# First loads on two queues, products of zeros ahead of the first turns, and constants made later

## The chip, the cores and the metric

The kernel runs on one core of a Trainium2 chip. The metric is the device time of one launch in microseconds (us), as the median of several runs.

## What is computed

An attention layer with random features is followed by a mixture of experts in which each token goes to one expert.

```python
# attention: q, k, v are (8 batches, 8 heads, 576 tokens, 64); omega is (128, 64)
proj = einsum('bhsd,md->bhsm', x * scale, omega)          # for q and for k
phi  = exp(h - max(h)) / sqrt(128)                        # h = proj - |x|^2/2
kv   = einsum('bhsm,bhsd->bhmd', k_p, v);  z = sum(k_p, axis=2)
num  = einsum('bhsm,bhmd->bhsd', q_p, kv); den = einsum('bhsm,bhm->bhs', q_p, z) + 1e-6
attn = num / den                                          # -> x: (4608, 512)
# experts: 8 of them, 512 -> 1024 -> 512
logits = x @ w_gate;  e = argmax(logits);  gate_w = softmax(logits)[e]
out = gate_w * (relu(x @ w1[e]) @ w2[e])
```

## The kernel before

**Units.** The attention stage (class `Attention`) goes through 72 units in a fixed order: for each of the 8 batches first a unit "rest" (head number -1, the last 64 tokens of all eight heads), then its heads 0 to 7 (512 tokens each). The text calls the first four units R, 0, 1 and 2. What one unit does:

- `unit_a1` (L136) calls `turn` (L146): TensorE transposes the unit's k and q, eight small products with the identity at L151, into the PSUM tile `tr`. There is a single buffer for all turned tiles (`room`, pool `ps_t`), so the next turn waits until the last one is copied out.
- `unit_a2`: VectorE copies `tr` to `th` (L157).
- `unit_b1`: TensorE multiplies `th` by the scaled omega, `omt`, into `pp` (L166). `pp` has two buffers.
- `unit_max`: VectorE takes the row maxima `mx` (L172).
- `unit_exp`: ScalarE takes the exponentials `kp` and `qp`, four instructions each (L180).
- The `qp` are turned back on TensorE (`t`, again L151) and copied by ScalarE to `qt` (L224). TensorE then makes the sums over k and v (`kf`, L206) and the results (`nu`).

**Order.** The loop in `run` (L293) is software-pipelined by hand. In iteration i it issues the turn of unit i+1, the products and maxima of unit i, the `qp` of unit i-1, the turning back of unit i-2, the `kf` of unit i-1, and the `kp` of unit i. The engines of the attention stage keep exactly the order in which the code issues (`manual_schedule`), each with its own queue, so an instruction that waits holds whatever follows it on its engine.

**Setup.** Ahead of the loop the code makes the identity, clears the buffers `xg` and `xgm` (L789), and makes the constants of the routing (`Routing.setup`, L404) on GpSimd, six of them with VectorE: L420 and L450 to L454. `Attention.__init__` loads omega twice (L75), turns it (L77) and scales it on ScalarE into `omt` (L79); it copies the identity 16 times into the gate table `G` (L89) and clears `rv` (L95), on GpSimd. The pool entry `tt` holds the turned omega too, so the first turn waits for L79.

**Loads.** `load(0)` puts every load of the first batch on SyncE's queue (SP), in this order: k and q of unit R (L111, two transfers each, for the two halves of the partitions), k and q of head 0, k and q of head 1, the gate weights into `G` (L124, two), v of heads 0 and 1, v of unit R into `rv` (two, which wait until GpSimd has cleared `rv`), and then k, q and v of heads 2 and 3, 4 and 5, 6 and 7. The loads of the second batch follow on the same queue.

The function `warm` (L688) issues products of a 128x128 bf16 tile of zeros with 512 columns of zeros. Nothing calls it in this kernel.

Of the kernel before, what the change touches and what calls it, by code (L numbers as in the profile page):

```python
# [30 lines left out]
NG = B // 2  # L31
GT = 2 * NJ + 1
NLT = NG * GT
# [7 lines left out]
SCALE = float(D) ** -0.25  # L41
# [16 lines left out]
class Attention:  # L58
    def __init__(self, tc, ctx, ps, io, q, k, v, omega, wg, xs, routing, ident):
        self.tc, self.nc = tc, tc.nc  # L60
        self.q, self.k, self.v, self.xs, self.routing, self.ident = q, k, v, xs, routing, ident
        nc = tc.nc
        pool = lambda n, b, **kw: ctx.enter_context(tc.tile_pool(name=n, bufs=b, **kw))
        self.cp = pool("at_c", 1)
        self.io, self.ps = io, ps
        self.open = ExitStack()
        self.pp = self.open.enter_context(tc.tile_pool(name="ps_a", bufs=2, space=PSUM))
        self.tt = self.open.enter_context(tc.tile_pool(name="ps_t", bufs=1, space=PSUM))
        self.wk = pool("at_wk", 2)
        self.xo = pool("at_x", 2)  # L70
        cp = self.cp

        om = self.wk.tile([P, 2, D], F32, name="om", tag="kp")
        for i in range(2):
            nc.sync.dma_start(om[:, i, :], omega)  # L75
        pt = self.tt.tile([P, 2, 512], F32, name="pt_om", tag="tt")
        nc.tensor.transpose(pt[:, 0, :P], om.rearrange("p a d -> p (a d)"), ident)  # L77
        self.om = cp.tile([P, M], F32, name="omt")
        nc.scalar.mul(self.om, pt[:, 0, :P], SCALE)  # L79

        self.G = cp.tile([P, H, W - 1], F32, name="G")
# [3 lines left out]
        nc.gpsimd.memset(self.eps, EPS)  # L85
        for a in range(2):
# [3 lines left out]
        self.wg = wg  # L90


        self.rv = [[cp.tile([P, NP, D], F32, name=f"rv{i}{a}") for a in range(2)] for i in range(2)]
        for t in self.rv[0] + self.rv[1]:
            nc.gpsimd.memset(t, 0.0)  # L95
        self.st, self.last = {}, {}

    def load(self, b):
# [7 lines left out]
        def rest(nms):  # L106
            for n, src in nms:
                rem = src[b, :, SM:, :].rearrange("(i a) p d -> a p i d", a=2)
                for a in range(2):
                    to = s["vr"][a] if n == 2 else s["kqr"][:, n]  # L110
                    nc.sync.dma_start(to[a * SR:(a + 1) * SR], rem[a])  # L111

        def main(nms, h):
            for nm, src in nms:
                nc.sync.dma_start(s[nm][:, h], src[b, h, :SM, :].rearrange("h (p j) d -> p h j d", j=NJ))
# [3 lines left out]
        if b == 0:  # L119
            main(kq, slice(0, 1))  # L120
            main(kq, slice(1, 2))
            for a in range(2):
                with nc.allow_non_contiguous_dma(reason="gate weights"):
                    nc.sync.dma_start(self.G[a * D:(a + 1) * D, :, D:], self.wg.rearrange("(h d) e -> d h e", d=D))  # L124
            main(v, slice(0, 2))
# [10 lines left out]
    def unit_a1(self, b, h):  # L136

        nc, s = self.nc, self.st[b]
        src = [s["kqr"][:, n] if h < 0 else s["kq"[n]][:, h] for n in range(2)]
        s[("tr", h)] = self.turn(self.next, [x[:, 2 * i:2 * i + 2, :].rearrange("p a d -> p (a d)")  # L140
                                                 for x in src for i in range(2)])
# [4 lines left out]
    def turn(self, pt, blocks):  # L146

        for n, x in enumerate(blocks):
            for a in range(2):
                r = slice(a * SR, (a + 1) * SR)  # L150
                self.nc.tensor.transpose(pt[:, a, n * SR:(n + 1) * SR], x[r], self.ident[r, r])  # L151
        return pt[:, :, :4 * SR].rearrange("p a (n t) -> p a n t", t=SR)
# [140 lines left out]
    def run(self, pre):  # L293
# [8 lines left out]
        for i in range(n):  # L302
# [32 lines left out]
            pre.ahead(i - n)  # L335
            if u1:
                self.next = self.room(f"tr_{i}")
                self.routing.product(self.next[:, 1, 256:])
# [56 lines left out]
class Routing:  # L395
# [8 lines left out]
    def setup(self):  # L404
# [8 lines left out]
        self.EX = t("rt_EX", [P, GT, E + 1])  # L413
        nc.gpsimd.memset(self.EX[:, :, E:], 1e-9)
        nc.gpsimd.memset(self.CU[:, 0, :], 0.0)

        self.iop = t("rt_iop", [P, P])
        self.iob = t("rt_iob", [P, P], BF16)
        nc.gpsimd.iota(self.iop, pattern=[[1, P]], base=0, channel_multiplier=0, allow_small_or_imprecise_dtypes=True)
        nc.vector.tensor_copy(self.iob, self.iop)  # L420
        self.rev = t("rt_rev", [P, E])
        nc.gpsimd.iota(self.rev, pattern=[[-1, E]], base=E, channel_multiplier=0, allow_small_or_imprecise_dtypes=True)
        self.zero = t("rt_zero", [P, P], BF16)
        nc.gpsimd.memset(self.zero, 0.0)
        self.ones = t("rt_ones", [P, P], BF16)
        nc.gpsimd.memset(self.ones, 1.0)
        self.tri = t("rt_tri", [P, P], BF16)
        nc.gpsimd.affine_select(out=self.tri, in_=self.ones, pattern=[[1, P]], compare_op=ALU.is_gt, fill=0.0,
                                base=0, channel_multiplier=-1)
        self.low = t("rt_low", [P, E, E])  # L430
        self.upp = t("rt_upp", [P, E, E])
# [6 lines left out]
        self.fold = t("rt_fold", [P, SR])  # L438
        nc.gpsimd.tensor_copy(self.fold, ident[:, :SR])
        nc.gpsimd.tensor_tensor(out=self.fold, in0=self.fold, in1=ident[:, SR:], op=ALU.add)  # L440
        idi = t("rt_id", [P, NG, GT], I32)
        nc.gpsimd.iota(idi[:, :, :GT - 1], pattern=[[2 * S, NG], [S, 2], [1, NJ]], base=0, channel_multiplier=NJ)
        for a in range(2):
            nc.gpsimd.iota(idi[a * SR:(a + 1) * SR, :, GT - 1:], pattern=[[2 * S, NG]], base=SM + a * S,
                           channel_multiplier=1)
        part = t("rt_part", [P, NLT], I32)
        self.ihi = t("rt_ihi", [P, NLT])
        self.ilo = t("rt_ilo", [P, NLT])
        flat = idi.rearrange("p g s -> p (g s)")
        nc.vector.tensor_single_scalar(part, flat, 6, op=ALU.logical_shift_right)  # L450
        nc.vector.tensor_copy(self.ihi, part)
        nc.vector.tensor_scalar_add(self.ihi, self.ihi, -float(NT // 64))
        nc.vector.tensor_single_scalar(part, flat, 63, op=ALU.bitwise_and)
        nc.vector.tensor_copy(self.ilo, part)  # L454
# [316 lines left out]
class Experts:  # L771
# [6 lines left out]
    def __init__(self, tc, ctx, rt, xs, w1, w2, out, ident, ps):  # L778
# [9 lines left out]
        for x in self.xg:  # L788
            self.nc.gpsimd.memset(x, 0.0)  # L789
# [373 lines left out]
```

## Time and profile before

| | us |
|---|---|
| median of 3 runs | 698.99 (698.91 to 699.36) |
| the profiled execution | 701.15 |
| its span, first to last instruction | 699.3 |
| what lies outside the span | 1.85 |

The attention stage fills about the first 250 us of the span, the experts the rest. In a timeline row stand the start, the duration, the engine, the line, the tile written and the tiles read, with shapes and the number of instructions merged into the row, and in brackets how long the engine was idle ahead of it and what ended that. A row of the DMA issues (SPq) shows the time in which the queue's engine was busy issuing, not the transfer itself.

### The profile page before, as it was taken

What the parts mean: (1) busy time and instruction counts of PE and PEld (TensorE: products, weight loads), DVE (VectorE), ACT (ScalarE), POOL (GpSimd) and SP (SyncE); (2) the same over time, 40 slices, a digit from 0 to 9 for tenths busy, and PEclk for the clock granted to TensorE, in tenths of its full rate; (3) what the DMA queues carried; (4) which work ended last, traced back from release to release, by engine and by line L of the source; (5) the groups of instructions that cost most, each with busy time, mean ns of one, the idle gap of its engine ahead of it and who ended that gap; (6) DMA issues with size and microseconds to landing.
All of it is one profiled execution on the core that took longest, in us unless ns stands there. A gap on an engine that the chain in (4) does not pass through costs nothing. (4 is left out here: it accounts for less than half of the span.)

```text
span 699.3 us, 19723 instructions
## 1 busy us (share of the span) xinstructions
PE 672.8 (96%) x7596; PEld 615.6 (88%) x7596; DVE 372.6 (53%) x738; ACT 359.9 (51%) x1096; POOL 272.4 (39%) x484
## 2 busy tenths in 40 slices
PE   5999999999999999999999999999999999999992
PEld 4999999999898977899899988999898999998891
DVE  4788888888887778532222253422383365422220
ACT  3999999999998944322212262222262263222120
POOL 6455547886887763222112202222231132122020
PEclk9999999999999999999999999999999999999997
DMA  5953836628492124851233247332267338422200
GB/s 160 269 168 114 268 88 191 209 76 252 138 373 73 34 76 138 286 179 64 93 97 108 91 158 241 108 106 71 84 205 242 108 112 320 138 79 61 78 18 21
DMA packets 92432, 99.57 MB, mean 142 GB/s; under 512 B 28943, under 2 KB 72975, under 8 KB 91665
## 3 DMA queue, kind: packets, MB, share of 16 engines
q1 hardware_dynamic: 85744, 78.91, 35.9%
q0 software_dynamic: 6560, 19.03, 8.2%
q8 instruction: 72, 1.18, 0.7%
q14 instruction: 56, 0.45, 0.2%
HBM read 71.06 MB, written 29.51 MB: 144 GB/s over the span
## 5 line engine op out<-in xcount | busy, mean ns | idle before, releaser
L943 PEld LDWEIGHTS p<-xb,w1p 128*128 128x128 f32 x1632 | 198.1, 192 | 1.7 <-issue 0.5
L943 PE MATMUL p<-xb,w1p 128*128 128x256 f32 x1632 | 198.9, 283 | 0.0
L868 PE MATMUL p<-w2p,hh 128*128 128x512 f32 x576 | 177.8, 390 | 0.0
L1014 POOL DMA_INDIRECT out_dram<-ys,idx x38 | 39.4, 1038 | 313.4 <-ACT ys L1013 201.3
L868 PEld LDWEIGHTS p<-w2p,hh 128*128 128x128 f32 x576 | 107.0, 188 | 21.3
L868 PE MATMUL p<-w2p,hl 128*128 128x512 f32 x312 | 117.7, 389 | 0.0
L1013 ACT ACTIVATE ys<-p,gt 128x512 f32<-128x512 f32 x38 | 26.1, 688 | 163.2 <-PE p L868 146.2
L999 DVE SCALAR_TENSOR_TENSOR hl<-p,hh 128x512 fp32r<-128x512 f32 x68 | 46.0, 688 | 80.5 <-ACT hh L995 78.3
L995 ACT ACTIVATE hh<-p 128x512 fp32r<-128x512 f32 x68 | 39.9, 598 | 91.5 <-PE p L943 91.5
L172 DVE TENSOR_REDUCE mx<-pp 128x8 f32<-128x1024 f32 x64 | 78.0, 1218 | 11.4 <-PE pp L166 10.7
L180 ACT ACTIVATE qp<-pp,mx 128x128 f32<-128x128 f32 x256 | 77.4, 438 | 0.0
L180 ACT ACTIVATE kp<-pp,mx 128x128 f32<-128x128 f32 x256 | 74.2, 387 | 4.6 <-DVE de L264 1.1
L166 PE MATMUL pp<-omt,th 64*128 64x128 f32 x1024 | 73.4, 285 | 0.0
L868 PEld LDWEIGHTS p<-w2p,hl 128*128 128x128 f32 x312 | 58.5, 188 | 12.2
L166 PEld LDWEIGHTS pp<-omt,th 64*128 64x128 f32 x1024 | 64.8, 194 | 0.0
L192 POOL TENSOR_TENSOR k<-kp 128x256 f32<-128x256 f32 x64 | 46.6, 728 | 27.7 <-ACT kp L180 21.8
L157 DVE COPY th<-tr 128x512 f32<-128x512 f32 x63 | 43.3, 687 | 6.8 <-PE tr L151 4.8
L927 DVE STREAM_TRANSPOSE xgm<-xq 128x512 f32<-128x512 f32 x18 | 18.9, 1086 | 51.3 <-DMA xq<-pair_rows 51.3
L255 PE MATMUL nu<-kva,qt 128*64 128x73 f32 x1008 | 46.0, 233 | 0.0
L224 ACT COPY qt<-t 128x512 f32<-128x512 f32 x64 | 42.0, 656 | 3.1 <-PE t L151 2.5
L255 PEld LDWEIGHTS nu<-kva,qt 128*64 128x64 f32 x1008 | 36.7, 136 | 4.2
L206 PE MATMUL kf<-kp,v 128*64 128x128 f32 x512 | 39.4, 275 | 0.0
(365 smaller groups left out, 1002.0 us busy)
## 6 DMA issues: line engine op xcount, KB each, us to landing
w1s<-in_moe_w_dram SPq DMA_DIRECT2D x5, 2048.0 KB, 8.8
w2s<-in_moe_w_dram SPq DMA_DIRECT2D x5, 2048.0 KB, 11.0
xq<-pair_rows SPq DMA_DIRECT2D x76, 128.0 KB, 2.9
v<-in_v_dram SPq DMA_DIRECT2D x32, 256.0 KB, 6.4
token_rows<-x SPq DMA_DIRECT2D x8, 1024.0 KB, 8.0
k<-in_k_dram SPq DMA_DIRECT2D x31, 256.0 KB, 5.2
q<-in_q_dram SPq DMA_DIRECT2D x31, 256.0 KB, 5.9
pair_rows<-xg SPq DMA_DIRECT2D x10, 512.0 KB, 2.8
```

The lines of the kernel that those rows point to most:

```text
L157: self.nc.vector.tensor_copy(t.rearrange("p n (a t) -> p a n t", a=2), s[("tr", h)])
L166: nc.tensor.matmul(o[:, a, n, :], t[r, n, :], self.om[r], start=True, stop=True)
L172: self.nc.vector.tensor_reduce(out=mx, in_=s[("pp", h)], axis=AX.X, op=ALU.max, negate=True)
L180: self.nc.scalar.activation(o[:, j, :], p[:, a, 2 * n + i, :], AF.Exp, bias=mx[:, a, 2 * n + i:2 * n + i + 1])
L192: nc.gpsimd.tensor_tensor(out=k2, in0=kp[:, :2, :], in1=kp[:, 2:, :], op=ALU.add)
L206: nc.tensor.matmul(pkv[c * D:(c + 1) * D, :M], vv, kk, start=n < 2, stop=n > 2)
L224: self.nc.scalar.copy(qt.rearrange("p n (a t) -> p a n t", a=2), s[("t2", h)])
L255: nc.tensor.matmul(o[r, j, :], qt[:, j, r], kva[:, h if h >= 0 else 2 * j + a, :], start=True, stop=True)
L868: self.nc.tensor.matmul(p, x, w[:, c, :], start=c == 0 and x is h and w is self.w2h, stop=c == self.NF - 1 and x is l)
L943: return [lambda w=w, x=x, c=c, n=n: self.nc.tensor.matmul(o, w[:, c, f], x[:, c, :], start=n == 0, stop=n == len(ops) - 1) for n, (w, x, ...
L995: self.nc.scalar.activation(a, self.p_1[g], AF.Relu)
L999: self.nc.vector.scalar_tensor_tensor(out=b, in0=self.p_1[g], scalar=0.0, in1=a.bitcast(F32), op0=ALU.max, op1=ALU.subtract)
```

## The change

Omega's second copy goes to ScalarE's queue, and so do, for the first batch alone, the q of unit R, the gate weights, the v of heads 0 and 1 and the v of unit R. Everything else stays on SP's queue, in its old order. The turning and scaling of omega moves behind the issue of the k and q of unit R. Products of zeros (`warm`) are issued on TensorE: five ahead of the turning of omega, two between the turned k and the turned q of unit R, three behind that q. On GpSimd the clearing of `rv` moves ahead of the copies into `G`; the routing's constants and the clearing of `xg` and `xgm` move out of the setup to the end of iteration 0 of `run`, and the six VectorE instructions among the constants move with them: they stand behind the maxima of unit R and ahead of the copy of unit 1's turn. The tile of zeros is cleared first of all. The attention's setup now stands inside the hand-ordered part too.

```diff
-        for i in range(2):
-            nc.sync.dma_start(om[:, i, :], omega)
-        pt = self.tt.tile([P, 2, 512], F32, name="pt_om", tag="tt")
-        nc.tensor.transpose(pt[:, 0, :P], om.rearrange("p a d -> p (a d)"), ident)
+        for i, eng in enumerate((nc.sync, nc.scalar)):
+            eng.dma_start(om[:, i, :], omega)
         self.om = cp.tile([P, M], F32, name="omt")
-        nc.scalar.mul(self.om, pt[:, 0, :P], SCALE)
+
+        def scaled():
+            self.idle = self.pair("idle")
+            self.routing.warm(self.idle[:, 0], 5)
+            pt = self.tt.tile([P, 2, 512], F32, name="pt_om", tag="tt")
+            nc.tensor.transpose(pt[:, 0, :P], om.rearrange("p a d -> p (a d)"), ident)
+            nc.scalar.mul(self.om, pt[:, 0, :P], SCALE)
+        self.scaled = scaled
...
+        self.rv = [[cp.tile([P, NP, D], F32, name=f"rv{i}{a}") for a in range(2)] for i in range(2)]
+        for t in self.rv[0] + self.rv[1]:
+            nc.gpsimd.memset(t, 0.0)
         for a in range(2):
             r = slice(a * D, (a + 1) * D)
             for h in range(H):
                 nc.gpsimd.tensor_copy(self.G[r, h, :D], ident[r, r])
...
-                    nc.sync.dma_start(to[a * SR:(a + 1) * SR], rem[a])
+                    (nc.scalar if b == 0 and n else nc.sync).dma_start(to[a * SR:(a + 1) * SR], rem[a])
...
-                nc.sync.dma_start(s[nm][:, h], src[b, h, :SM, :].rearrange("h (p j) d -> p h j d", j=NJ))
+                (nc.scalar if b == 0 and nm == "v" and not h.start else nc.sync).dma_start(s[nm][:, h], src[b, h, :SM, :].rearrange("h (p j) d -> p h j d", j=NJ))
...
         rest(((0, self.k), (1, self.q)))
         if b == 0:
+            self.scaled()
             main(kq, slice(0, 1))
             main(kq, slice(1, 2))
             for a in range(2):
                 with nc.allow_non_contiguous_dma(reason="gate weights"):
-                    nc.sync.dma_start(self.G[a * D:(a + 1) * D, :, D:], self.wg.rearrange("(h d) e -> d h e", d=D))
+                    nc.scalar.dma_start(self.G[a * D:(a + 1) * D, :, D:], self.wg.rearrange("(h d) e -> d h e", d=D))
...
         s[("tr", h)] = self.turn(self.next, [x[:, 2 * i:2 * i + 2, :].rearrange("p a d -> p (a d)")
-                                                 for x in src for i in range(2)])
+                                                 for x in src for i in range(2)],
+                                     (0, 2, 0, 3) if b == 0 and h < 0 else (0, 0, 0, 0))
...
-    def turn(self, pt, blocks):
+    def turn(self, pt, blocks, busy=(0, 0, 0, 0)):
 
         for n, x in enumerate(blocks):
             for a in range(2):
                 r = slice(a * SR, (a + 1) * SR)
                 self.nc.tensor.transpose(pt[:, a, n * SR:(n + 1) * SR], x[r], self.ident[r, r])
+            self.routing.warm(self.idle[:, 0], busy[n])
...
             self.unit_sum(*u)
             pre.ahead(i - n)
+            if i == 0:
+                self.routing.constants()
+                pre.clear()
...
+    def constants(self):
+        nc, ident = self.nc, self.ident
         nc.gpsimd.memset(self.EX[:, :, E:], 1e-9)
         nc.gpsimd.memset(self.CU[:, 0, :], 0.0)
...
         nc.vector.tensor_copy(self.iob, self.iop)
...
+        nc.vector.tensor_single_scalar(self.part, flat, 6, op=ALU.logical_shift_right)
+        nc.vector.tensor_copy(self.ihi, self.part)
         nc.vector.tensor_scalar_add(self.ihi, self.ihi, -float(NT // 64))
...
+        nc.vector.tensor_single_scalar(self.part, flat, 63, op=ALU.bitwise_and)
+        nc.vector.tensor_copy(self.ilo, self.part)
...
-        for x in self.xg:
-            self.nc.gpsimd.memset(x, 0.0)
+        self.clear = lambda: [self.nc.gpsimd.memset(x, 0.0) for x in self.xg]
...
+        zero = cp.tile([P, P], BF16, name="zero")
+        nc.gpsimd.memset(zero, 0.0)
         ident = cp.tile([P, P], F32, name="ident")
         make_identity(nc, ident)
         rt = Routing(tc, ctx, xs, ident)
+        rt.zero = zero
...
-            at = Attention(tc, c2, ps, io, q, k, v, omega, wg, xs, rt, ident)
-            rt.open(ps, "nu")
             with sched():
+                at = Attention(tc, c2, ps, io, q, k, v, omega, wg, xs, rt, ident)
+                rt.open(ps, "nu")
                 at.run(ex)
```

## Rows read from the trace of the kernel before

**Rows 1.** Stretches: length, busy time of each engine, PEclk, DMA share, GB/s.

```profile
0.00:5.00 5.00, 0.81 (x4) 0.39 (x4) 0.61 (x1) 1.56 (x2) 4.35 (x21) 1.00 0.23 51
5.00:10.00 5.00, 3.33 (x29) 2.77 (x31) 2.50 (x7) 0.00 (x0) 4.71 (x26) 1.00 0.67 158
...
40.00:50.00 10.00, 9.76 (x207) 8.96 (x205) 8.40 (x17) 9.88 (x38) 4.75 (x11) 1.00 0.69 212
```

**Rows 2.** Timeline of units R and 0, up to the first exponentials.

```profile
0.81 1.28 ACT L79 ACT_TABLE_LOAD   x1 [0.81 <-PEq L1150]
...
3.36 0.44 PE L77 MATMUL pt_om<-ident,om 128*128 128x128 f32 x1 [3.36 <-DMA om<-in_omega_dram]
...
4.97 0.90 PE L151 MATMUL tr_first<-ident,kqr 64*128 64x64 f32 x4 [0.32 <-DMA kqr<-in_k_dram]
...
6.70 0.47 PE L151 MATMUL tr_first<-ident,kqr 64*128 64x64 f32 x3 [0.83 <-DMA kqr<-in_q_dram]
...
7.21 0.69 DVE L157 COPY th_-1_229<-tr_first 128x512 f32<-128x512 f32 x1 [0.57 <-PE tr_first L151]
...
7.95 0.48 PE L151 MATMUL tr_second<-ident,k 64*128 64x64 f32 x4 [0.78 <-DVE th_-1_229 L157]
...
8.43 2.02 PE L166 MATMUL pp_-1_242<-omt,th_-1_229 64*128 64x128 f32 x16
...
10.51 1.23 DVE L172 TENSOR_REDUCE mx_-1_251<-pp_-1_242 128x8 f32<-128x1024 f32 x1 [1.13 <-PE pp_-1_242 L166]
...
11.77 1.14 ACT L180 ACTIVATE kp_-1_254<-pp_-1_242,mx_-1_251 128x128 f32<-128x128 f32 x4 [7.64 <-DVE mx_-1_251 L172]
```

**Rows 3.** Timeline of ScalarE: `kp` of unit 0, `qt` of R, `kp` of 2.

```profile
14.00 1.14 ACT L180 ACTIVATE kp<-pp,mx 128x128 f32<-128x128 f32 x4
...
17.37 0.59 ACT L224 COPY qt_-1_360<-t_-1_351 128x512 f32<-128x512 f32 x1 [1.19 <-PE t_-1_351 L151]
...
22.23 1.14 ACT L180 ACTIVATE kp<-pp,mx 128x128 f32<-128x128 f32 x4 [0.55 <-DVE mx L172]
```

**Rows 4.** The stretch between those two `kp`: length, ScalarE busy, PEclk, DMA share, GB/s.

```profile
14.00:22.23 8.23, 5.70 (x20) 1.00 0.97 267
```

**Rows 5.** Timeline of TensorE and VectorE in that stretch.

```profile
13.78 0.48 PE L151 MATMUL tr<-ident,k 64*128 64x64 f32 x4 [1.08 <-DMA k<-in_k_dram]
...
17.01 1.22 DVE L172 TENSOR_REDUCE mx<-pp 128x8 f32<-128x1024 f32 x1 [1.19 <-PE pp L166]
...
19.21 1.60 PE L166 MATMUL pp<-omt,th 64*128 64x128 f32 x16
...
22.26 1.11 PE L166 MATMUL pp<-omt,th 64*128 64x128 f32 x16
```

**Rows 6.** Timeline of SP's queue: the issues of the first loads.

```profile
0.81 0.89 SPq L75 DMA_DIRECT2D om<-in_omega_dram  x2
1.74 1.41 SPq L111 DMA_DIRECT2D kqr<-in_k_dram  x2
3.20 1.27 SPq L111 DMA_DIRECT2D kqr<-in_q_dram  x2
...
6.58 1.29 SPq L124 DMA_DIRECT2D G<-in_moe_w_gate_dram  x2
...
9.21 1.29 SPq L111 DMA_DIRECT2D rv<-in_v_dram  x2
10.56 0.60 SPq L115 DMA_DIRECT2D k<-in_k_dram  x1
```

**Rows 7.** VectorE alone in the stretch that holds its six constants (columns as rows 4).

```profile
3.30:7.10 3.80, 1.73 (x6) 1.00 0.59 146
```

**Rows 8.** Timeline of TensorE: a stream of products with 512 columns.

```profile
284.56 5.63 PE L868 MATMUL p<-w2p,hl 128*128 128x512 f32 x24
```

**Rows 9.** Stretches behind TensorE's last product (columns as rows 1).

```profile
685.00:686.00 1.00, 0.49 (x3) 0.07 (x1) 0.00 (x0) 0.34 (x1) 0.00 (x0) 1.00 0.08 16
...
689.00:690.00 1.00, 0.00 (x0) 0.00 (x0) 0.00 (x0) 0.00 (x0) 0.00 (x0) 0.61 0.00 0
```

More of the change, by code (lines that the diff above doesn't have):

```diff
@@ L85, in __init__ @@
         nc.gpsimd.memset(self.eps, EPS)
+        self.wg = wg
+        self.rv = [[cp.tile([P, NP, D], F32, name=f"rv{i}{a}") for a in range(2)] for i in range(2)]
+        for t in self.rv[0] + self.rv[1]:
+            nc.gpsimd.memset(t, 0.0)
         for a in range(2):
@@ L89, in __init__ @@
                 nc.gpsimd.tensor_copy(self.G[r, h, :D], ident[r, r])
[L90 to L95, printed above, removed]
         self.st, self.last = {}, {}
@@ L413, in setup @@
         self.EX = t("rt_EX", [P, GT, E + 1])
+        self.iop = t("rt_iop", [P, P])
+        self.iob = t("rt_iob", [P, P], BF16)
+        self.rev = t("rt_rev", [P, E])
+        self.ones = t("rt_ones", [P, P], BF16)
+        self.tri = t("rt_tri", [P, P], BF16)
+        self.low = t("rt_low", [P, E, E])
+        self.upp = t("rt_upp", [P, E, E])
+        self.fold = t("rt_fold", [P, SR])
+        self.idi = t("rt_id", [P, NG, GT], I32)
+        self.part = t("rt_part", [P, NLT], I32)
+        self.ihi = t("rt_ihi", [P, NLT])
+        self.ilo = t("rt_ilo", [P, NLT])
+    def constants(self):
+        nc, ident = self.nc, self.ident
         nc.gpsimd.memset(self.EX[:, :, E:], 1e-9)
         nc.gpsimd.memset(self.CU[:, 0, :], 0.0)
-        self.iop = t("rt_iop", [P, P])
-        self.iob = t("rt_iob", [P, P], BF16)
         nc.gpsimd.iota(self.iop, pattern=[[1, P]], base=0, channel_multiplier=0, allow_small_or_imprecise_dtypes=True)
         nc.vector.tensor_copy(self.iob, self.iop)
-        self.rev = t("rt_rev", [P, E])
         nc.gpsimd.iota(self.rev, pattern=[[-1, E]], base=E, channel_multiplier=0, allow_small_or_imprecise_dtypes=True)
-        self.zero = t("rt_zero", [P, P], BF16)
-        nc.gpsimd.memset(self.zero, 0.0)
-        self.ones = t("rt_ones", [P, P], BF16)
         nc.gpsimd.memset(self.ones, 1.0)
-        self.tri = t("rt_tri", [P, P], BF16)
         nc.gpsimd.affine_select(out=self.tri, in_=self.ones, pattern=[[1, P]], compare_op=ALU.is_gt, fill=0.0,
                                 base=0, channel_multiplier=-1)
-        self.low = t("rt_low", [P, E, E])
-        self.upp = t("rt_upp", [P, E, E])
         nc.gpsimd.memset(self.low, 1.0)
@@ L437, in setup @@
                                 base=0, channel_multiplier=0)
-        self.fold = t("rt_fold", [P, SR])
         nc.gpsimd.tensor_copy(self.fold, ident[:, :SR])
         nc.gpsimd.tensor_tensor(out=self.fold, in0=self.fold, in1=ident[:, SR:], op=ALU.add)
-        idi = t("rt_id", [P, NG, GT], I32)
-        nc.gpsimd.iota(idi[:, :, :GT - 1], pattern=[[2 * S, NG], [S, 2], [1, NJ]], base=0, channel_multiplier=NJ)
+        nc.gpsimd.iota(self.idi[:, :, :GT - 1], pattern=[[2 * S, NG], [S, 2], [1, NJ]], base=0, channel_multiplier=NJ)
         for a in range(2):
-            nc.gpsimd.iota(idi[a * SR:(a + 1) * SR, :, GT - 1:], pattern=[[2 * S, NG]], base=SM + a * S,
+            nc.gpsimd.iota(self.idi[a * SR:(a + 1) * SR, :, GT - 1:], pattern=[[2 * S, NG]], base=SM + a * S,
                            channel_multiplier=1)
[L446 to L451, printed above, removed]
+        flat = self.idi.rearrange("p g s -> p (g s)")
+        nc.vector.tensor_single_scalar(self.part, flat, 6, op=ALU.logical_shift_right)
+        nc.vector.tensor_copy(self.ihi, self.part)
         nc.vector.tensor_scalar_add(self.ihi, self.ihi, -float(NT // 64))
-        nc.vector.tensor_single_scalar(part, flat, 63, op=ALU.bitwise_and)
-        nc.vector.tensor_copy(self.ilo, part)
+        nc.vector.tensor_single_scalar(self.part, flat, 63, op=ALU.bitwise_and)
+        nc.vector.tensor_copy(self.ilo, self.part)
     def open(self, ps, tag):
```

## The prediction

> **What bounds the kernel now.** The change touches only the first 20 us or so, so I first ask whether a microsecond won there reaches the end. The table of stretches says it does: from 40 to 50 us ScalarE is busy 9.88 of 10 us [rows 1]. The units pass one after the other at the pace of that engine, nothing there is tied to the clock on the wall, and the experts start when the attention is through. What counts is the moment from which ScalarE runs without gaps.
>
> The timeline shows that moment: the `kp` of unit 2 at 22.23 [rows 3]. Ahead of it the reader is to see three stretches. Up to 11.77 ScalarE has nothing to do, because a chain runs through the loads, the turn, the copy, the products and the maxima of unit R [rows 2]. TensorE waits in turn for omega (3.36), for k (4.97) and for q (6.70) [rows 2], and the DMA engines are busy only 0.23 of the first 5 us [rows 1]: the loads are late because one queue issues them one by one, 0.45 us for each omega, about 0.7 us for each half of k and q [rows 6]. Then, from the `kp` of unit 0 at 14.00 to that of unit 2 at 22.23, ScalarE is busy 5.70 of 8.23 us [rows 4]; it waits for TensorE (the turned `t`, 1.19 us) [rows 3]. TensorE is late there for two reasons. It waited 1.08 us for the k of unit 2, issued only at 10.56, behind the issue of `rv` [rows 5, 6]. And it is slow: sixteen products of L166 take 2.02 us at 8.43, 1.60 us at 19.21 and 1.11 us at 22.26 [rows 2, 5]. The clock column says 1.00 in all these stretches [rows 1, 4], but the pace is that of the lower level (1.2 GHz) until about 20 us and of the upper one (2.4 GHz) behind it. The durations decide here. Ahead of the rise the engine had worked from 13.78 on with only short pauses.
>
> **The change, part by part.** I follow the chain of unit R with TensorE at the lower level.
>
> *Loads on two queues.* SP issues omega (0.45 us) and the two k (1.41) from 0.81 on, done at 2.7; in the trace the second k lands 1.8 us behind the end of its issue (3.15 to 4.97) [rows 2, 6], so now at 4.5. ScalarE issues the other omega and the two q (0.45 + 1.27) by 2.5; the second q landed 2.2 us behind its issue (4.47 to 6.70), so now at 4.8. An issue from ScalarE does not occur in the trace; I take SP's durations. Below: no cheaper than these. Above: the same row kinds up to twice as long if two queues hinder each other, which would put k at 5.6 and cost 1.1 us.
>
> *Products of zeros.* Twenty-four products with 512 columns take 5.63 us at the upper level, 0.235 each [rows 8]; with the ratio 2.02/1.11 that is 0.43 at the lower. Another shape of bf16 with 512 columns the trace doesn't have; the range is 0.235 to 0.43. Five of them fill 1.05 to 3.2, in which TensorE waited for omega anyway (until 3.36 before): nothing. Turned omega then takes 0.44, to 3.65, and its scaling is done at about 4.1, ahead of the k. The k turns run 4.5 to 4.75 (eight turns take 0.48, 7.95 to 8.43 [rows 2]). Two products end at 5.6; they hide a q that lands up to then, otherwise they cost 0.8. The q turns end at 5.85, the copy `th` starts 0.25 later and ends at 6.8 (0.69 [rows 2]). Three products end at 7.15, so they hold the second turn by 0.35 us.
>
> *Chain to the maxima.* Second turn to 7.65; products of R 7.65 to 9.5; maxima start 2.08 behind the start of the products (8.43 to 10.51 [rows 2]), so at 9.75, and end at 10.95. Before: 11.74. Won so far: 0.8 us.
>
> *The constants on VectorE.* The six instructions, 1.73 us [rows 7], lay in VectorE's idle time before the first copy. Now they are queued behind the maxima of R, and behind them wait the copy of unit 1's turn and with it the maxima of unit 0, for which ScalarE waits. They read what GpSimd makes; GpSimd's whole setup, 4.35 + 4.71 us of work [rows 1], ends by about 10 in either order, so VectorE needn't wait for it. The copy starts at 12.7 and ends at 13.35, the maxima of unit 0 at 14.55. The `kp` of unit 0 comes at 14.55, against 14.00: **0.55 later**, the early loads notwithstanding.
>
> *What follows.* From there the gaps go. The k and q of heads 2 and 3 are issued at 4.8 instead of 10.56, and landed 3.2 us behind that (13.78) [rows 5, 6]; at 8 to 9 they are far ahead of unit 2's turn, which now waits until 13.4 for the copy of unit 1's, since both use the one room. TensorE by then has worked from 4.5 to about 11 nearly without a pause, so I take its clock to have risen by about 10. Then that turn takes 0.25 and the products of unit 1 take 1.1; the maxima of unit 1 end at 16.5, the `qt` of R can start at 16.6, the maxima of unit 2 end at 19.8: each is ready as ScalarE comes to it. ScalarE's work between the two `kp` is 5.70 us [rows 4], some 0.5 less if the ends of its instructions overlap as they do in streams (`kp` 14.00 to `qp` 15.02 while the row shows 1.14 [rows 3]). The `kp` of unit 2 comes between 19.75 and 20.25, against 22.23: **2.0 to 2.5 us won; I take 2.2.**
>
> *The rest, at nothing.* The clearing of `xg` and the constants on GpSimd lie ahead of its first sum, which needs the `kp` of unit 0; GpSimd is free at 10, 4 us earlier. The scaling of omega is needed at 7.65. The second batch's loads are issued some 6 us earlier and come behind the first batch's on the same queue. The copies into `G`, now behind the clearing of `rv`, are read only behind the `kp` of unit 0.
>
> By the Trainium skill ("ScalarE: Activation LUTs", Step-by-step: what each stage is for) the activation table is loaded right before the first instruction that needs it. The trace shows the load at 0.81, 1.28 us, on an idle engine [rows 2], which decides nothing about issues standing ahead of it. Placed first, it would put the second q at 6.1, 0.5 us behind the two products, and take 0.3 to 0.5 us from the 2.2.
>
> **Sum.** Span 699.3 - 2.2 = 697.1; with the 1.85 us around it 698.95, against 701.15 for the profiled execution. The median of the runs lies 2.16 below that execution, so the forecast is 696.8. If the clock rises by 8.5, the products of R take 1.1 instead of 2.0: 3.1 won, 695.9. With late issues, 1.1 less at worst: 697.9.
>
> **The rivals.**
>
> *The clock does not rise early, or falls again.* Behind unit 0's products TensorE would stand idle from about 10 to 12.7 and work sparsely until 16. At the end of the kernel it did its last product in the first half of the stretch from 685, did none behind it, and the clock fell within the stretch from 689 [rows 9]; here products come again after 2.7 us, but few. If the lower level holds until 20 as before, the products of unit 1 end at 15.9 and those of unit 2 at 20.2, its maxima at 21.6: 0.6 won, 698.4. Speaking for it: the clock rose only after a long dense stretch before. The Trainium skill ("TensorE: Matmul & The Clock Gate", Part 4: PE-mode transpose) says that transposes don't count as work for the gate; by that the turns here bring nothing to the rise and only the ten products and L166 do. No row separates the two.
>
> *The sharing brings nothing*, because the transfers land no earlier from a second queue. Then q comes at 6.7 as before, three products hold the second turn to 8.25 and the `kp` of unit 0 comes at 15.5; without the later gaps 1.1 us is still won: 697.9. Against it: the DMA engines were idle three quarters of the time [rows 1].
>
> *ScalarE is held by its own issues: slower.* It issues eight transfers; five (gate weights, v, `rv`) come behind the scaling of omega, 1.29 + 0.6 + 1.29 = 3.2 us (the v priced like the k at 10.56 [rows 6]), from 3.9 to 7.1. Its first `kp` is due at 10.95, 3.8 us later, and another 1.6 us are spare between that and the `kp` of unit 0 (14.55, less two groups of 1.02). So issues up to 2.7 times as long as SP's cost nothing; from 3.4 times on all that was won is gone. At four times they end at 16.7, 5.75 behind 10.95: less the 1.6 and the 2.2 that is 2.0 slower, 701.0. For it: no row shows what an issue costs on ScalarE. Against: the DMA engines that it feeds are not full then (0.23, 0.67 [rows 1]).
>
> *What is won is lost downstream*: some later point waits for something that didn't move. 699.0. The waits of the attention stage show none.
>
> **How the numbers follow.** Forecast 0.64 (695.9 to 697.3, up to 697.9 with late issues); clock 0.15 (698.4, from 697.4 to 698.8); sharing 0.07; ScalarE held 0.07; lost downstream 0.07. 0.2% is 1.4 us, about what a measurement of this kernel tells from no change; so "faster" is below 697.6. To it go the forecast nearly whole (0.62), a fourth of the clock's cases (0.04) and a fourth of the sharing's (0.02): 0.68. Slower: ScalarE held, 0.07. Same: 0.25. The range 695.6 to 698.7 takes in the forecast with its bounds, the clock and the sharing, and leaves out the last two, 0.14.
>
> **What would show it.** Five products at 1.05; turned k at about 4.5; first `kp` near 11; `kp` of unit 0 no earlier than 14, behind six VectorE instructions; then ScalarE gapless and `kp` of unit 2 near 20; L166 in 1.1 us from unit 1 on. Wrong, if L166 still takes 2 us at 14, if ScalarE's issues reach past 10, or if the `kp` of unit 0 comes well before 14 (then the constants cost less than I say).

## The result: 5.9 us slower, and the profile after

The changed kernel takes 704.9 us as the median of 6 runs (703.96 to 705.36), beside 698.96 for the kernel before (698.9 to 699.36): a ratio of 1.0081, with a 95% interval of 1.007 to 1.0092. The forecast was 696.8. Executions of one and the same kernel differ here by some microseconds (those of the kernel before lay between 697.2 and 702.5 in all that were timed), so below each time stands beside runs of the kernel before on the same chip.

The profiled execution of the changed kernel took 704.19 us with a span of 702.3; the one of before had 701.15 and 699.3, and lies 2.2 above its median, so the two traces differ by 3.0 us of span where the medians differ by 5.9. The first view is ScalarE's timeline in the changed kernel (start, duration, engine, line; ACTq is ScalarE issuing a transfer):

```profile
1.27 1.38 ACTq L116 DMA_DIRECT2D kqr<-in_q_dram  x2
2.68 1.28 ACT L83 ACT_TABLE_LOAD   x1 [2.68 <-issue]
3.97 0.28 ACT L83 ACTIVATE omt<-pt_om 128x128 f32<-128x128 f32 x1
8.81 2.36 ACTq L130 DMA_DIRECT2D G<-in_moe_w_gate_dram  x2
12.01 0.39 ACTq L120 DMA_DIRECT2D v<-in_v_dram  x1
13.56 2.60 ACTq L116 DMA_DIRECT2D rv<-in_v_dram  x2
16.21 1.14 ACT L188 ACTIVATE kp_-1_242<-pp_-1_230,mx_-1_239 128x128 f32<-128x128 f32 x4 [11.96 <-DMA v<-in_v_dram]
...
18.22 1.19 ACT L188 ACTIVATE kp<-pp,mx 128x128 f32<-128x128 f32 x4
...
25.34 1.14 ACT L188 ACTIVATE kp<-pp,mx 128x128 f32<-128x128 f32 x4 [0.49 <-DVE mx L180]
```

Omega is scaled at 4.25. Then ScalarE computes nothing for 12 us. Its five later issues come out at 8.81 (and a second gate transfer behind that), 12.01 and 13.56, and its first `kp` at 16.21, against 11.77 before [rows 2]. The bracket of that row names a DMA, not the maxima. The row of the maxima shows that they were not the reason (VectorE's timeline, with the first constant and the copy behind the last):

```profile
10.27 1.23 DVE L180 TENSOR_REDUCE mx_-1_239<-pp_-1_230 128x8 f32<-128x1024 f32 x1 [0.26 <-PE pp_-1_230 L174]
11.41 0.22 DVE L443 CAST rt_iob<-rt_iop 128x128 bf16<-128x128 f32 x1
...
12.37 0.68 DVE L165 COPY th<-tr 128x512 f32<-128x512 f32 x1
```

They ended at 11.50, so ScalarE was held 4.7 us beyond them. Further on the `kp` of unit 0 comes at 18.22 (14.00 before, [rows 3]), and that of unit 2 at 25.34 (22.23 before). The 3.1 us by which it is late reach the end. The last product of the experts starts, in TensorE's timeline of before, at 685.11,

```profile
685.11 0.39 PE L868 MATMUL p<-w2p,hl 128*128 128x512 f32 x1
```

and in that of the changed kernel 2.95 later:

```profile
688.06 0.39 PE L878 MATMUL p<-w2p,hl 128*128 128x512 f32 x1
```

TensorE's timeline shows the second loss. In this execution the clock had risen early, as forecast, since the products of R take 1.13 us at 9.09 against 2.02 before [rows 2]. Then TensorE ran out of work, and the products of unit 1 take 2.08 again:

```profile
1.07 2.31 PE L703 MATMUL idle<-zero 128*128 128x512 bf16 x5 [1.07 <-POOL zero L1137]
...
5.44 0.47 PE L158 MATMUL tr_first<-ident,kqr 64*128 64x64 f32 x3 [0.73 <-DMA kqr<-in_k_dram]
...
9.09 1.13 PE L174 MATMUL pp_-1_230<-omt,th_-1_217 64*128 64x128 f32 x16
...
18.44 2.08 PE L174 MATMUL pp<-omt,th 64*128 64x128 f32 x16 [4.86 <-ACT qp_-1_319 L188]
```

Here the clock column shows it too (stretches of 1 us: length, busy time of PE, PEld, DVE, ACT, POOL, then PEclk, DMA share and GB/s):

```profile
15.00:16.00 1.00, 0.00 (x0) 0.00 (x0) 0.00 (x0) 0.00 (x0) 0.00 (x0) 0.97 1.07 256
16.00:17.00 1.00, 0.00 (x0) 0.00 (x0) 0.00 (x0) 0.79 (x4) 0.00 (x0) 0.50 0.95 201
...
22.00:23.00 1.00, 1.00 (x14) 0.67 (x15) 0.00 (x0) 1.00 (x5) 0.00 (x0) 0.61 0.69 168
23.00:24.00 1.00, 1.00 (x22) 0.97 (x22) 0.69 (x1) 1.00 (x6) 0.81 (x2) 1.00 1.00 339
```

The engine did nothing from 13.6 to 18.44, the granted clock fell to the lower level (0.50 of full speed) at about 16, and it rose again between 22 and 23.

What ScalarE waited for is found in the compiled program, in which every instruction stands with the semaphores for which it waits. In this program each transfer signals its completion on one of eight semaphores (DMAHW0 to 7). They are handed out in turn, over both queues together, and an issue that gets one of them again first waits until the transfer that had it has landed. For the changed kernel, ScalarE's and SP's instructions in order:

```
ACT 4  L83  ACTIVATE omt            [waits PE]
ACT 5  L130 DMA G                   [waits DMAHW2]
ACT 6  L130 DMA G                   [waits DMAHW3]
ACT 7  L120 DMA v heads 0-1         [waits DMAHW5]
ACT 8  L116 DMA rv00                [waits DMAHW7, Pool]
ACT 9  L116 DMA rv01                [waits DMAHW1, Pool]
ACT 10 L188 ACTIVATE kp of R        [waits DVE]
SP 7  k heads 2-3 [DMAHW2]    SP 11 q heads 4-5 [DMAHW6]
SP 8  q heads 2-3 [DMAHW3]    SP 12 v heads 4-5 [DMAHW7]
SP 9  v heads 2-3 [DMAHW4]    SP 13 k heads 6-7 [DMAHW0]
SP 10 k heads 4-5 [DMAHW5]    SP 14 q heads 6-7 [DMAHW1]
```

The five issues have DMAHW2, 3, 5, 7 and 1: the semaphores that SP's k and q of heads 2 and 3, k and v of heads 4 and 5 and q of heads 6 and 7 have just taken. ScalarE therefore can't issue the gate weights, which nobody needs yet, before 256 KB of k have landed, nor the second half of `rv` before the q of heads 6 and 7 has, and its exponentials stand behind all that. The trace keeps the semaphores' events too, and with them the moment at which each of those transfers had landed (the last of its sixteen events):

| ScalarE's issue | the transfer it waits for | landed at (us) | the issue starts at (us) |
|---|---|---|---|
| first G | k of heads 2 and 3 | 8.79 | 8.81 |
| second G | q of heads 2 and 3 | 10.55 | 10.57 |
| v of heads 0 and 1 | k of heads 4 and 5 | 11.98 | 12.01 |
| first half of rv | v of heads 4 and 5 | 13.48 | 13.56 |
| second half of rv | q of heads 6 and 7 | 15.49 | 15.56 |

Each issue starts 0.02 to 0.08 us behind the landing, so the waits are these. They go the other way as well: SP's q of unit R of the second batch, which has nothing to do with the gate weights, waits for ScalarE's load of them (view of SP's waits: in total, times, longest):

```profile
SPq L116 <- DMA G<-in_moe_w_gate_dram: 1.3, 2, 0.8
```

SP's timeline shows those loads going out ahead of ScalarE's:

```profile
5.06 0.43 SPq L120 DMA_DIRECT2D k<-in_k_dram  x1
5.53 0.47 SPq L120 DMA_DIRECT2D q<-in_q_dram  x1
...
6.56 0.47 SPq L120 DMA_DIRECT2D k<-in_k_dram  x1
...
7.58 0.47 SPq L120 DMA_DIRECT2D v<-in_v_dram  x1
...
8.61 0.65 SPq L120 DMA_DIRECT2D q<-in_q_dram  x1
```

### The profile page after: what moved, and what is told of

It reads as the page before. It is cut to its first block, busy times and chain, and to the rows that moved or that the text cites. A ratio compares the mean times of both kernels' runs of the same rounds, so it can differ in the third digit from the quotient of the medians.

```text
span 702.3 us, 19738 instructions
## 1 busy us (share of the span) xinstructions
PE 673.6 (96%) x7606; PEld 613.8 (87%) x7606; DVE 372.0 (53%) x738; ACT 358.9 (51%) x1096; POOL 270.7 (39%) x484
```

## The experiments

None of the kernels leaves a part of the computation out. Each median stands beside that of the kernel before on the same chip. The ratio and its 95% interval are worked out from all these runs and need not be the quotient of the two medians.

**The kernel before, again.**

> The kernel before, once more. Its profiled execution took 701.15 us, 2.2 above the median of its runs, while that of the changed kernel lies within the range of its runs. Theory: the profiled execution of before happened to have a late rise of TensorE's clock (the sixteen L166 products slow until about 20 us), and an execution of the usual time shows the rise earlier: kp of unit 2 near 20 instead of 22.23, span near 697. Rival: the profile itself costs the old kernel 2 us, or the 2 us lie in the experts' stage: then the head looks as before, kp of unit 2 at 22.2, in a span of 699.

699.37 us (697.19 to 700.73, 10 runs) beside 699.85, ratio 0.9994 (0.9979 to 1.001). Its profiled execution took 697.51, and it shows why executions differ. The products of unit 1 run at the fast pace already, and the `kp` of unit 2 comes 2.45 us earlier than in the execution on which the prediction rests [rows 3, 5]:

```profile
14.66 1.11 PE L166 MATMUL pp<-omt,th 64*128 64x128 f32 x16
...
19.78 1.23 ACT L180 ACTIVATE kp<-pp,mx 128x128 f32<-128x128 f32 x4
```

So the moment at which the clock rises differs from one execution of this kernel to the next, and with it some 2.3 us of the start (the first `kp` differs by only 0.19). The execution that I had worked from was a late one.

**Five of ScalarE's eight issues back on SP** (omega and the q of R stay on ScalarE).

```diff
-                    (nc.scalar if b == 0 and n else nc.sync).dma_start(to[...], rem[a])
+                    (nc.scalar if b == 0 and n == 1 else nc.sync).dma_start(to[...], rem[a])
...
-                (nc.scalar if b == 0 and nm == "v" and not h.start else nc.sync).dma_start(s[nm][:, h], ...)
+                nc.sync.dma_start(s[nm][:, h], ...)
...
-                    nc.scalar.dma_start(self.G[...], ...)
+                    nc.sync.dma_start(self.G[...], ...)
```

> The changed kernel with the five later transfers (gate weights, v of heads 0 and 1, v of unit R) back on SP's queue; ScalarE issues only omega and the two q. Theory: ScalarE stood from 4.25 to 16.2 us because each of those five issues waited until a transfer issued later from SP had landed (they share completion semaphores); then its first kp comes at 11.4, right behind the maxima of R, the kp of unit 0 at 14.2, of unit 2 near 19.8, no fall of TensorE's clock, and the time is 5 to 6 us below the changed kernel's: about 699.3. Rival: the loss comes from the products of zeros or from the constants on VectorE: then the time stays within 1 us of 704.9.

699.23 us (697.88 to 701.43, 10 runs) beside 699.85, ratio 1.0002 (0.9983 to 1.002). The loss is gone: the ratio falls from 1.0081 to 1.0002. The first `kp` starts at 12.80, right behind the maxima, and that of unit 2 at 21.03, 4.3 earlier than in the changed kernel. So the loss hangs on the five issues.

**All eight on ScalarE, but nothing that waits ahead of them**: omega is scaled by VectorE, and the five stand ahead of the k and q of heads 0 and 1 in the code.

```diff
-            nc.scalar.mul(self.om, pt[:, 0, :P], SCALE)
+            nc.vector.tensor_scalar_mul(self.om, pt[:, 0, :P], SCALE)
...
-            main(kq, slice(0, 1))
-            main(kq, slice(1, 2))
             for a in range(2):
...
         rest(((2, self.v),))
+        if b == 0:
+            main(kq, slice(0, 1))
+            main(kq, slice(1, 2))
```

> The changed kernel with all eight transfers still on ScalarE's queue, but the scaling of omega on VectorE, and the five later transfers issued ahead of the k and q of heads 0 and 1: they get the semaphores of omega, k and q of unit R, not those of SP's later loads. Theory (waits for shared semaphores): all eight issues are done by 8 us, the first kp comes at 11.4 to 12, and the time is within 1 us of five_on_sp. Rival (issues from ScalarE are slow in themselves, or two queues hinder each other): the first kp still comes behind 13 us and the time stays above 702.

700.39 us (699.05 to 702.05, 10 runs) beside 699.85, ratio 1.0021 (1.0004 to 1.0038). All eight are issued by 9.08 and the first `kp` comes at 11.73. The median lies 1.2 above that of the kernel with five issues on SP, where the theory allowed 1. So it is not that ScalarE issues, nor how many transfers; it is for what the issues wait. This kernel made two edits at once, so each was also made alone.

**The order of the code alone.**

> The changed kernel with one thing moved: k and q of heads 0 and 1 are issued behind the v of unit R in the code, so the five later issues of ScalarE stand ahead of four SP loads. The compiled list of waits gives the five the same completion semaphores as in the changed kernel (those of SP's k and q of heads 2 and 3, k and v of heads 4 and 5, q of heads 6 and 7). Theory (the five issues wait for those transfers): as the changed kernel, first kp of unit R near 16.2, 703.5 to 705. Rival (what cured scale_on_vector was that the five stood ahead of k and q of heads 0 and 1 in the code, so that SP's large loads took no place in front of them): first kp near 12, about 700.

705.28 us (702.74 to 706.3, 5 runs) beside 698.91, ratio 1.0079 (1.0053 to 1.0105): as slow as the changed kernel. The list of waits is that of the changed kernel too, and so is ScalarE's timeline:

```profile
3.95 0.28 ACT L83 ACTIVATE omt<-pt_om 128x128 f32<-128x128 f32 x1
9.29 1.53 ACTq L128 DMA_DIRECT2D G<-in_moe_w_gate_dram  x2
11.54 0.39 ACTq L120 DMA_DIRECT2D v<-in_v_dram  x1
13.77 2.45 ACTq L116 DMA_DIRECT2D rv<-in_v_dram  x2
16.26 1.14 ACT L189 ACTIVATE kp_-1_242<-pp_-1_230,mx_-1_239 128x128 f32<-128x128 f32 x4 [12.04 <-DMA v<-in_v_dram]
```

**The scaling alone.**

> The changed kernel with one thing moved: the scaling of omega goes to VectorE, the code's order of the loads stays. The five issues no longer stand behind a ScalarE instruction that waits for TensorE, and the compiled list gives them semaphores of early transfers (none, omega, a half of q of R, a k or q of R, the first G). Theory (the hold is the wait for the shared semaphores, and the scaling on ScalarE is what moves the five behind SP's large loads in their turn): five issues done by about 9.5, first kp near 11.7, 699.5 to 701. Rival (the order of the loads was what counted): first kp near 16, 703.5 to 705.

701.17 us (698.88 to 702.99, 10 runs) beside 698.91, ratio 1.0023 (1.0004 to 1.0043). In its list the first of the five waits for nothing and the others for DMAHW0, 2, 5 and 3, whose transfers land early: ScalarE is through at 8.49.

```profile
2.65 1.32 ACTq L130 DMA_DIRECT2D G<-in_moe_w_gate_dram  x2
4.08 0.58 ACTq L120 DMA_DIRECT2D v<-in_v_dram  x1
5.31 3.18 ACTq L116 DMA_DIRECT2D rv<-in_v_dram  x2
8.53 1.28 ACT L188 ACT_TABLE_LOAD   x1 [8.53 <-DMA rv<-in_v_dram]
12.26 1.14 ACT L188 ACTIVATE kp_-1_242<-pp_-1_230,mx_-1_239 128x128 f32<-128x128 f32 x4 [2.46 <-DVE mx_-1_239 L180]
```

With the scaling on ScalarE the five stand behind an instruction that waits for TensorE, and by the numbers of the list they get their semaphores only after twelve of SP's loads of heads have had theirs; with the scaling elsewhere they come far ahead in that turn. The code's order of the loads has no part in it. Between the two kernels lie 4.1 us. The first `kp` is 0.6 later than the theory had it, and the clock of this execution rose and fell again without any hold: the products of unit 0 take 1.11 us at 11.10, those of unit 1 2.08 at 14.49, and the column shows 0.50 from 15 to 17. In the kernel with both edits, whose TensorE paused as long ahead of them (1.70 us there, 1.64 here), the products of unit 1 took 1.16.

**The ten products of zeros taken out**, once of the kernel with five issues on SP and once of the changed kernel.

```diff
-            self.routing.warm(self.idle[:, 0], 5)
...
-                                     (0, 2, 0, 3) if b == 0 and h < 0 else (0, 0, 0, 0))
+                                     (0, 0, 0, 0))
```

> five_on_sp without the ten products of zeros. Theory: they bring the clock up near 9 us for 0.7 us of delay; without them the first maxima come 0.5 us earlier at the lower pace or about the same, the clock rises only at 17 to 20, the kp of unit 2 comes 1 to 1.5 us later and the time is about 1 us above five_on_sp. Rival: the clock rises as early without them; then the time is 0 to 0.7 us below five_on_sp.

697.2 us (696.52 to 700.04, 10 runs) beside 699.85, ratio 0.9973 (0.9956 to 0.999), the first kernel that beats the one before. The `kp` of unit 0 comes at 13.21 instead of 15.49. TensorE's timelines show from where: with the products,

```profile
5.92 0.47 PE L158 MATMUL tr_first<-ident,kqr 64*128 64x64 f32 x3 [1.26 <-DMA kqr<-in_k_dram]
6.33 1.04 PE L703 MATMUL idle<-zero 128*128 128x512 bf16 x2
7.29 0.47 PE L158 MATMUL tr_first<-ident,kqr 64*128 64x64 f32 x4
7.70 1.46 PE L703 MATMUL idle<-zero 128*128 128x512 bf16 x3
...
9.58 1.92 PE L174 MATMUL pp_-1_230<-omt,th_-1_217 64*128 64x128 f32 x16
```

and without:

```profile
5.24 0.68 PE L158 MATMUL tr_first<-ident,kqr 64*128 64x64 f32 x7 [0.58 <-DMA kqr<-in_k_dram]
...
7.19 2.02 PE L174 MATMUL pp_-1_220<-omt,th_-1_207 64*128 64x128 f32 x16
...
12.87 2.02 PE L174 MATMUL pp<-omt,th 64*128 64x128 f32 x16
```

The k of R landed 0.68 us later in the first of these (5.24 to 5.92). The two products then hold the turns of q to 7.29, and the three hold the second turn, so that the products of R start 2.4 us later. What the ten were put there for comes late for R in this execution: its products take 1.92 with them and 2.02 without, those of unit 0 1.11 and 2.02. The five traces with all ten have 1.13 to 2.02 for R and 1.11 to 1.53 for unit 0; the seven without any, those of before among them, have 2.02 for R and 1.27 to 2.02 for unit 0. So with the ten the clock tends to be up earlier, for R only in some executions.

> The changed kernel without its ten products of zeros; the five issues stay on ScalarE behind the scaling of omega. Theory: ScalarE's queue is held until about 15.5 to 16 by waits for SP's later transfers, so that an earlier th or maxima help nothing: first kp at 15.5 or later, time within 1.2 us of the changed kernel's 704.9. Rival: the products are the changed kernel's loss: 2 us or more below it.

703.82 us (703.15 to 704.51 but for one run of 752.14, 8 runs) beside 700.14, ratio 1.0048 (1.003 to 1.0065). The first `kp` still comes at 16.34 and that of unit 2 at 25.64 (25.34 with the products), so at the start of these two executions the products' 2 us are hidden behind the hold. The median is only 1.1 below 704.9, as the theory says, but beside the runs of before on its own chip the loss has shrunk: 1.0048 against 1.0081, with intervals that don't overlap. Whether that is the products or the runs of before, whose median was 698.96 there and 700.14 here, is open.

**Only the five products ahead of omega**, with five issues on SP.

```diff
-                                     (0, 2, 0, 3) if b == 0 and h < 0 else (0, 0, 0, 0))
+                                     (0, 0, 0, 0))
```

> five_on_sp with the five products of zeros ahead of omega kept, the two and three inside the first turn left out. Theory: the five lie in a wait for the loads and the activation table and cost nothing, while the two and three hold the copy th and the second turn by 1.9 us at the lower clock; the first copy comes at 6 us as without any zeros, the kp of unit 0 at 13.2, and the time is within 0.7 us of five_on_sp_no_zeros, about 697.2 against before's 699.4 to 699.9 (before varies by 4 us between executions), and not the 699.2 of five_on_sp. Rival: all ten act together on the clock, or the five cost as well: then it lies at 698 or above.

698.57 us (696.79 to 699.46, 11 runs) beside 700.14, ratio 0.9972 (0.9956 to 0.9988), the ratio of the kernel without any.

```profile
1.06 2.31 PE L703 MATMUL idle<-zero 128*128 128x512 bf16 x5 [1.06 <-POOL zero L1137]
...
5.23 0.69 PE L158 MATMUL tr_first<-ident,kqr 64*128 64x64 f32 x7 [0.59 <-DMA kqr<-in_k_dram]
...
13.11 1.11 PE L174 MATMUL pp<-omt,th 64*128 64x128 f32 x16
```

They cost the start nothing: the turns start at 5.23 and the products of R at 7.18, as without them. The time itself, 698.57, is what the rival said (698 or above), on a chip on which before was 0.3 slower; the ratios are alike, the medians' distances from before are not (1.6 here, 2.65 above), so a cost of up to a microsecond elsewhere is not excluded. That the five raise the clock sooner isn't shown: the products of unit 1 take 1.11 us here at 13.11 and 2.02 at 12.87 above, but in the next kernel, which has no products of zeros, 1.16 at 12.88. The `kp` of unit 2 comes 0.4 us earlier (18.75 against 19.17).

**The constants early**: without products, five issues on SP, and GpSimd makes the routing's constants right behind the clearing of `rv`, ahead of the copies into `G`.

```diff
+        self.routing.constants()
         for a in range(2):
             r = slice(a * D, (a + 1) * D)
...
-                self.routing.constants()
                 pre.clear()
```

> five_on_sp_no_zeros with the routing's constants made ahead of the gate table's copies on GpSimd and ahead of the first copy on VectorE, instead of behind the maxima of R. Theory: the six instructions, 0.95 us when they run back to back, lie on VectorE ahead of the copy of unit 1's turn; taken away, the kp of unit 0 comes 0.25 us earlier if the products of unit 0 are then late at the lower clock, up to 0.95 if the clock is up: 0.2 to 0.9 us faster than 697.2. Rival: the k of heads 2 and 3 or the products bind instead: no difference.

696.96 us (696.0 to 698.03, 8 runs) beside 700.14, ratio 0.9957 (0.9939 to 0.9974), the fastest of all. VectorE does the six in its idle time ahead of the first copy (its timeline, with the first two of them, then the copy):

```profile
2.88 0.29 DVE L443 CAST rt_iob<-rt_iop 128x128 bf16<-128x128 f32 x1 [2.88 <-POOL rt_iop L442]
5.22 0.18 DVE L461 TENSOR_SCALAR rt_part<-rt_id 128x36 int32<-128x36 int32 x1 [2.06 <-POOL rt_id L458]
...
6.10 0.68 DVE L166 COPY th_-1_228<-tr_first 128x512 f32<-128x512 f32 x1
```

The `kp` of unit 0 comes at 12.89, 0.3 earlier than with the constants behind the maxima. That these 0.3 us show in the median is not sure: the intervals of this kernel and of the one without the move overlap.

**The sharing alone**: the kernel before with omega's second copy and the q of R on ScalarE's queue, and nothing else.

```diff
-            nc.sync.dma_start(om[:, i, :], omega)
+            eng.dma_start(om[:, i, :], omega)
...
-                    nc.sync.dma_start(to[...], rem[a])
+                    (nc.scalar if b == 0 and n == 1 else nc.sync).dma_start(to[...], rem[a])
```

> The kernel before with one edit: omega's second copy and the two q of unit R on ScalarE's queue. Theory: the q of R lands about 1.2 us earlier, th comes at 6 instead of 7.1, SP issues all later loads 1.7 us earlier except those behind rv (still cleared at 8.9 to 9.9), kp of unit 0 about 1 us earlier: 0.5 to 1.2 us faster than before. Rival: all of the 2.6 us between before and five_on_sp_no_zeros come from it: then it equals that one, 697.2; or nothing comes from it, 699.4 to 699.9.

700.24 us (698.82 to 702.21, 11 runs) beside 700.14, ratio 1.0006 (0.9991 to 1.0021): nothing won. The copy `th` starts at 6.54 instead of 7.21 [rows 2], yet the turn of unit 2 still waits for its k, which stands behind `rv` on SP's queue, and `rv` behind GpSimd's clearing:

```profile
13.87 0.34 PE L151 MATMUL tr<-ident,k 64*128 64x64 f32 x4 [2.13 <-DMA k<-in_k_dram]
```

In the better kernels `rv` is cleared earlier, and the turn of unit 2 no longer waits for k: in the one without products that k is issued at 8.46 instead of 10.54, and the turn starts at 12.10, behind a copy. So their 2 to 3 us need more than the sharing. The earlier clearing is the part that the traces point at; no kernel makes it without the sharing, or alone, so how much of the gain it would give by itself is not shown.

**All eight on ScalarE with short waits, and no products.**

> As scaling_alone, and without the ten products of zeros: all eight transfers stay on ScalarE. Theory (the eight issues cost nothing once their waits are short, and the five products inside the first turn cost 2): first kp of unit R 10 to 10.7, kp of unit 0 near 13, 697 to 698, as the kernel with three issues on ScalarE and no products (697.2). Rival (ScalarE's five issues still cost the start 1 us or more even with short waits): 698.5 to 700.

699.81 us (698.14 to 700.94, 10 runs) beside 698.91, ratio 1.0008 (0.9992 to 1.0023). At the start this is what the theory says: the first `kp` at 10.85, that of unit 0 at 13.54 and that of unit 2 at 19.45, all within 0.35 of the kernel with three issues on ScalarE. The time is the rival's. By the starts of the `kp`, its profiled execution loses 0.35 us more at about 104 and 0.7 around 206, and then 1.8 in the passage from the attention to the experts, where the clock fell for some 4 us:

```profile
244.00:246.00 2.00, 2.00 (x26) 1.86 (x28) 0.93 (x4) 0.39 (x2) 0.49 (x3) 0.72 0.00 0
246.00:248.00 2.00, 2.00 (x20) 1.70 (x18) 1.18 (x7) 0.53 (x2) 1.16 (x3) 0.50 0.00 0
248.00:250.00 2.00, 2.00 (x12) 1.52 (x11) 0.91 (x4) 0.00 (x0) 2.00 (x4) 0.93 0.18 62
```

Why a kernel with the same start should lose there is open. The clock fell in that passage in 5 of the 13 profiled executions (in all three with the scaling on VectorE, and in two others), behind a pause of about 1.5 us that the undisturbed ones have as well.

## Why the prediction was wrong

**What bounds the kernel** was read rightly. In the two traces the shift of the start goes through to the end, 3.11 us at the `kp` of unit 2 and 2.95 at the last product.

**The step that failed** is the cost of ScalarE's five later issues. The prediction priced them by SP's durations, 3.2 us from 3.9 to 7.1, and found 3.8 us of room. The issues themselves are no longer than SP's (0.39 for v in the row at 12.01; 1.32 for the two `G` where they don't wait, at 2.65 above). What they wait for was left out, and "ScalarE is held by its own issues" was only asked with longer issues, though the trace of before has issues that wait for another transfer (view of SP's waits, as above):

```profile
SPq L115 <- DMA k<-in_k_dram: 0.7, 1, 0.7
```

What the term should have held is the landing of SP's loads, the last of them at 15.49. The issues ended at 16.16 instead of 7.1, and the first `kp` came at 16.21 instead of 10.95. The rival with 0.07 was the one that occurred, larger than its 701.0 and through another mechanism: the waits for shared semaphores, shown by the landings in the trace and by the pair of kernels with the order alone and the scaling alone. Its end of the issues, 16.7, came close to the 16.16 by luck; what it lacks to 704.9 are the stretch behind the hold and the step to the median, both below.

The Trainium skill ("DMA: Bandwidth & Descriptors", Issuing engines are not separate DMA queues) says that a second issuing engine saves only the time that it takes to initiate a transfer. The runs agree that this is little: the sharing alone moved `th` by 0.67 us and the median by nothing that shows.

**The clock.** "Risen by about 10" came true (products of R at 9.09 in 1.13 us). That was luck in part: with the same turns and products at the same times, the kernel with the order alone took 2.02 for them. It didn't last, and the rival "falls again" occurred, here within the pause that the hold makes; the kernel with the scaling alone shows that the clock can fall there without a hold. From the forecast 20.0 to the measured 25.34 for the `kp` of unit 2, the `kp` of unit 0 accounts for 3.7 (14.55 to 18.22) and the stretch behind it for 1.6 (5.5 to 7.1), in which the products of unit 1 took 2.08 instead of 1.1. Together 5.3, which is the span's miss of 5.2 (697.1 to 702.3). What the rule of the Trainium skill on transposes ("TensorE: Matmul & The Clock Gate", Part 4: PE-mode transpose) would make of the rise no run separates, for turns and products come mixed in all of them.

**The step from the profiled execution to the median** failed as well. I took 2.16 us off because the runs of before lay that far below the profiled execution, and 2.2 more because the clock would rise earlier. The second profile of before has the `kp` of unit 2 at 19.78 without the change, since its clock rose earlier, so most of one gain was counted twice. The changed kernel's median lies 0.7 above its profiled execution. 5.2 + 2.2 + 0.7 are the 8.1 us between 696.8 and 704.9.

**Sizes.** Five products ahead at nothing: right (2.31 us for five, 0.43 each behind one another, as estimated). 2 + 3 products at 0.35: in kernels that are not held they move the products of R by 2.4 us, of which 0.7 go with a later k; the forecast had q landing as late as their end, and without them the eight turns run through from 5.24, so q was there and the two products were pure delay. The k of R at 4.5: it came at 5.44, and at 5.1 to 5.9 in the others, within the bound of 5.6 but for one. That bound is mis-added: issues twice as long from 0.81 on, and 1.8 to the landing, put k at 6.3 and cost 1.8, not 1.1, and the 697.9 that rests on it should be 698.6. Constants on VectorE at 1.73: 0.96 (11.41 to 12.37). Most of them were shorter here, the first one 0.22 us where it took 0.61 before; why, no run shows. The table load stood at 2.68, behind three issues, where the prediction's own times put it, and not at the first place, which it weighed and didn't take; omega was scaled at 4.25 instead of 4.1 and nobody waited for it.

**The pieces without the failed one** do win: five issues on SP, no products of zeros at all and early constants give 0.9957 of the time before, some 3 us, where the prediction said 2.2 for the whole change.

## What to carry to other kernels

An issue on a compute engine's queue costs what it waits for, not its duration: list those waits in the compiled program, and put on a compute engine only issues whose semaphores belong to transfers that have landed when it gets there, ahead of any instruction that waits. Even so placed, the five won nothing here (1.0008, against 0.9973 with them on SP). Work that fills an idle engine can be free only ahead of a wait that it doesn't outlast. Before a shift of 2 us is forecast from one profiled execution, look at a second one, and don't take the distance to the median off a time from which the same cause has been taken already.

## What the hardware showed unexpectedly

The clock of TensorE rises at different moments in executions of one kernel: the products of unit 1 took 2.02 us at 14.88 in one profile of the kernel before and 1.11 at 14.66 in another, and the executions of this kernel lay between 697.2 and 702.5 us. It fell to the lower level within a pause of 4.9 us (2.08 us for the products behind it), and in another kernel behind one of 1.64 us, where a third with a pause of 1.70 us stayed at the upper level. In some executions it fell in the passage to the experts, where TensorE pauses for about 1.5 us, and in others with the same pause it did not. In the first microseconds the column shows 1.00 while the products run at half pace [rows 1, 2, 4]; in the fall at 16 it shows 0.50 with the same pace.
